# Moving the decay polynomial to GpSimd and regrouping the first products behind the attention

## The chip, the cores and the metric

One core of a Trainium2 chip runs the whole program in one launch. TensorE (PE) does the matmuls, VectorE (DVE), ScalarE (ACT) and GpSimd (POOL) work on data in SBUF, and DMA queues (here those of SP and ACT) move data from and to HBM. The time is that of the device in microseconds, from launch to end. The profile shows one execution of the same program.

## What is computed

A forgetting attention over 4 x 8 heads of 576 positions and 64 dimensions, then two feed-forward layers over the 2304 tokens; in short:

```python
log_f = np.log(np.clip(f, 0.0001, 1.0))
cum = np.cumsum(log_f, axis=-1)
decay = cum[:, :, :, None] - cum[:, :, None, :]
scores = np.where(causal, -1e9, q @ k.T / sqrt(D) + decay)
x = softmax(scores) @ v                 # to 2304 x 512
h = x @ w_in;  x = (h * tanh(log1p(exp(h)))) @ w_out
out = ((x @ w1) * (x @ w2)) @ w3 @ w_out2
```

All numbers are float32 to the reader, but the matmuls work on pairs: every operand is split into a hi part and a lo part (what the rounding of hi left), and three products hi*hi, hi*lo, lo*hi (`MM_PAIRS`) stand for one.

## The kernel before

**The start.** `phase_a` writes an order out by hand for ScalarE, VectorE and SP (`manual_schedule`); GpSimd's order is left to the scheduler. The weights arrive as 64-bit words. Each block of 128x512 goes through four steps: a load on SP (`cv_load`, L122), a rescaling of the exponent on ScalarE (`cv_exp`, L133), three bit operations on VectorE (`cv_bits`, L141 to L143, together a conversion), and the split: a cast to hi on ScalarE (L98) and a subtraction for lo on VectorE (L102), or later on GpSimd (L112). The list `first` holds ten such blocks in this order: t00, o0 to o3, t01, o4 to o7 (t is w3, o is the second w_out); `NEAR` of them are loaded ahead of the decays, and the first softmax is put behind the conversion with index `HOLD`. The blocks that come after (w3h of 44 us among them) are converted in the slots.

The decays are made by `decay_log` and `decay_rows`: the clipped f is split into mantissa and exponent, log of the mantissa is a polynomial in z = s*s (L264 to L267 on VectorE, ten operations on 128x144), then come the term of the exponent (L268, L269), a running sum (L279, a scan) and its rounding to pairs (L282 to L288). Four stores on SP (L290) write them to `cum_scr`, from which `load_cum` (L342 to L347) brings them as rows of `aug`, two more contraction rows of the attention's score products on TensorE (L371).

**The slots.** From there the attention runs in slots, in which TensorE alternates scores (L371, L374), transposes (L438, L442), products with v (L472) and a filler: the units of w3 times w_out (L521) and of the first layer's x @ w_in (L552). `misc` holds loads and splits by slot; up to slot 2 they are kept behind the last load of the start (`go_sp`).

**The boundary.** The filler ends with the first eight of the layer's products done for most tokens; the last block of tokens runs in `first_layer` by a scheme with seven products o = 1 to 7 for each of eight units m (Strassen and Winograd). Each product takes an x operand (TX, made by `x_operands`: sums on VectorE, cast on ScalarE, lo on VectorE L955) and a weight: products 1, 2 and 4 use the weights `wi` as they are, products 5, 6, 3 and 7 use `sp`, sums of weight quarters made on VectorE (`s_sums`, L1122 to L1127) and split by `s_build` (hi on ScalarE L1134, lo on VectorE L1135). The results are added into C: by ScalarE for products 1, 5 and 6 (L1070 to L1074) and by VectorE for 2, 3 and 7 (L1076 to L1080). `m_order` gives the order of the products; the operands are made ahead or behind a product by `hook`.

Of the kernel before, what the change touches and what calls it, by code (L numbers as in the profile page):

```python
# [43 lines left out]
NEAR = 4  # L44
# [31 lines left out]
class Kernel:  # L76
# [172 lines left out]
    def decay_log(self):  # L249
# [14 lines left out]
        dve.tensor_scalar(q, z, 1.0 / 17, None, ALU.mult)  # L264
        for k in (15, 13, 11, 9, 7, 5, 3):
            dve.scalar_tensor_tensor(q, q, 1.0 / k, z, ALU.add, ALU.mult)
        dve.scalar_tensor_tensor(q, q, 1.0, s, ALU.add, ALU.mult)  # L267
# [4 lines left out]
    def decay_rows(self, between, after):
# [38 lines left out]
    def zeros(self):  # L311

        nc = self.nc
        for i in range(2):
            nc.vector.memset(f32(self.aug[i]), 0.0)
            for r in (0, 64):
                nc.gpsimd.memset(f32(self.aug[i][r:r + 4, 0:S]), 1.0)
                nc.gpsimd.memset(f32(self.aug[i][r:r + 4, S:LAST if r else 2 * S]), 1.0)
            nc.gpsimd.memset(f32(self.aug[i][64:68, 2 * S:KQ]), 1.0)
            nc.gpsimd.memset(self.raw[i][0:64, 2 * S:2 * S + 64], 0.0)  # L320
            nc.gpsimd.memset(self.raw[i][64:128, LAST:2 * S], 0.0)
            nc.gpsimd.memset(self.pt4[i][64:128], 0.0)
            nc.gpsimd.memset(self.vb[i][64:128], 0.0)
# [277 lines left out]
    def phase_a(self):  # L601
# [16 lines left out]
        def go(i):  # L618
            self.cv_exp(first[i][0])
            self.last = self.cv_bits(first[i][0])  # L620

# [3 lines left out]
        self.consts()  # L625
# [1 line left out]
        with self.tc.manual_schedule(engines={getattr(mybir.EngineType, e) for e in ("Activation", "DVE", "SP")}):
# [708 lines left out]
```

## Time and profile before

| what | value |
|---|---|
| median of three runs | 924.03 us (926.38, 923.31, 924.03) |
| profiled execution | 920.79 us, of which 919.0 us span |
| mean granted TensorE clock | 0.991 |
| TensorE busy | 873.7 us (95%) |
| VectorE, ScalarE, GpSimd busy | 688.1, 483.3, 166.2 us |

The busy shares are averages over the whole span. To judge a change in one stretch, read the stretch itself: which engine was idle there, what ended its idle time, and what that releaser had been doing until then. A timeline line gives the begin of a group of like instructions, its length, the engine, the line of the kernel, the tiles written and read, and in brackets how long the engine stood idle before and whose work ended that. The end of a matmul is modelled, so the begin of the next one is the better mark.

### The profile page before, as it was taken

The page shows a single profiled execution, that of the slowest core. Times are in us where ns is not written, and L with a number is a line of the kernel's source. Part 1 is how long each engine was busy: PE and PEld are TensorE (multiplying, and loading weights), DVE is VectorE, ACT ScalarE, POOL GpSimd, SP SyncE. Part 2 cuts the span into 40 slices and gives each one's busy share as a digit, 9 for nine tenths or more (in the row PEclk, how much of TensorE's full clock was granted, in tenths as well). Part 3 has the DMA queues.
Part 4 walks back from the last instruction along what each step waited for, and adds up shares of the span by engine and source line. Part 5 has one row for each costly group of instructions (what it writes and reads, how often), then busy time and mean ns, then how long its engine had stood idle before and what let it go on. Part 6 is the DMA issues. An engine that isn't in the chain of part 4 may idle for free.

```text
span 919.0 us, 17491 instructions
## 1 busy us (share of the span) xinstructions
PE 873.7 (95%) x6338; PEld 806.1 (88%) x6338; DVE 688.1 (75%) x1361; ACT 483.3 (53%) x1035; POOL 166.2 (18%) x253
## 2 busy tenths in 40 slices
PE   2799999999999989799999999999999999999998
PEld 1577778888888758799999999999999999999998
DVE  8987796744767676788888889888788887544483
ACT  3766667655556454655645455455784545322152
POOL 4043333325778740000000000000000000000000
PEclk9899999999999999999999999999999999999999
DMA  6965567757788872244475549988986555555552
GB/s 186 273 193 171 174 195 223 214 159 231 247 274 277 286 239 89 70 138 138 138 229 161 184 165 337 368 316 296 413 303 190 153 168 169 161 164 166 174 166 78
DMA packets 129191, 190.12 MB, mean 207 GB/s; under 512 B 12352, under 2 KB 70736, under 8 KB 129104
## 3 DMA queue, kind: packets, MB, share of 16 engines
q1 hardware_dynamic: 114608, 172.66, 58.2%
q10 hardware_dynamic: 14496, 16.33, 5.8%
q8 instruction: 50, 0.82, 0.4%
q14 instruction: 37, 0.30, 0.1%
HBM read 131.44 MB, written 57.52 MB: 206 GB/s over the span
## 4 chain that ended last, share of the span: by engine, by line
PE 63%; DMA 7%; DVE 7%; POOL 5%; issue 2%; ACT 1%; SPq 0%; ACTq 0%; DVEq 0%; POOLq 0%
PE ps_x L993 15%; PE ps_x L1065 14%; PE ps_z L1065 7%; PE ps_l L552 6%; PE ps_z L993 6%; PE ps_y L993 6%; PE ps_y L1065 3%; DMA ws<-ws 2%; PE ps_s L371 2%; PE ps_s L472 2%; POOL pt L849 2%; DMA ws<-pt 1%; PE ps_t L438 1%; POOL pt L848 1%; DVE TX L955 1%
## 5 line engine op out<-in xcount | busy, mean ns | idle before, releaser
L552 PE MATMUL ps_l<-x,wi 128*128 128x288 f32 x696 | 103.2, 302 | 0.6 <-ACT h L556 0.6
L552 PEld LDWEIGHTS ps_l<-x,wi 128*128 128x128 f32 x696 | 94.8, 190 | 5.7 <-issue 2.8
L954 ACT CAST g_h<-y 128x576 fp32r<-128x576 f32 x96 | 63.6, 675 | 55.0 <-PE ps_x L993 26.1
L993 PE MATMUL ps_x<-g_h,ws 128*128 128x288 f32 x512 | 91.5, 297 | 0.9 <-ACT g_h L954 0.7
L955 DVE TENSOR_TENSOR g_l<-y,g_h 128x576 fp32r<-128x576 f32 x96 | 72.3, 753 | 16.1 <-ACT g_h L954 15.3
L401 ACT ACTIVATE P<-P,sum 128x256 f32<-128x256 f32 (+3 forms) x112 | 70.5, 631 | 24.7 <-DVE sum L391 14.6
L993 PEld LDWEIGHTS ps_x<-g_h,ws 128*128 128x128 f32 x512 | 75.8, 189 | 1.8 <-ACT g_h L954 1.2
L391 DVE CUSTOM_DVE_ANT_0 P<-ps_s,m 128x256 f32<-128x256 f32 (+2 forms) x96 | 48.4, 553 | 18.9 <-PE ps_s L371 18.9
L993 PE MATMUL ps_x<-g_l,ws 128*128 128x288 f32 x256 | 55.2, 297 | 0.5 <-DVE g_l L955 0.5
L453 DVE COPY pt<-ps_t 128x128 f32<-128x128 f32 (+1 forms) x64 | 29.7, 485 | 34.5 <-PE ps_t L438 33.8
L1065 PE MATMUL ps_x<-T,gs 128*128 128x288 f32 x384 | 53.8, 295 | 0.9 <-ACT Cg L1070 0.9
L371 PE MATMUL ps_s<-raw 64*128 64x128 f32 (+3 forms) x256 | 46.6, 476 | 8.3 <-DMA raw<-in_qk_dram 5.9
L1065 PE MATMUL ps_x<-T,ws 128*128 128x288 f32 x384 | 53.8, 295 | 0.0
L1065 PEld LDWEIGHTS ps_x<-T,gs 128*128 128x128 f32 x384 | 51.8, 188 | 1.1 <-ACT Cg L1070 1.1
L1065 PEld LDWEIGHTS ps_x<-T,ws 128*128 128x128 f32 x384 | 51.9, 188 | 0.0
L521 PE MATMUL ps_l<-wo,w3h 128*128 128x512 f32 x128 | 45.3, 423 | 5.2 <-DVE wo L102 4.0
L954 ACT CAST h_h<-ab 128x576 fp32r<-128x576 f32 x48 | 31.7, 673 | 34.0 <-PE ps_x L993 19.9
L993 PE MATMUL ps_x<-h_h,ws 128*128 128x288 f32 x256 | 46.3, 297 | 1.5 <-DMA ws<-ws 1.4
L955 DVE TENSOR_TENSOR h_l<-ab,h_h 128x576 fp32r<-128x576 f32 x48 | 35.9, 754 | 15.6 <-ACT h_h L954 15.5
L472 PE MATMUL ps_s<-pt,va 128*64 128x320 f32 (+3 forms) x384 | 45.0, 383 | 0.0
L438 PE MATMUL ps_t<-ident,P 128*128 128x128 f32 x288 | 40.2, 275 | 2.5 <-ACT pt L453 2.2
L993 PEld LDWEIGHTS ps_x<-g_l,ws 128*128 128x128 f32 x256 | 41.2, 189 | 1.0 <-DVE g_l L955 1.0
(278 smaller groups left out, 2180.0 us busy)
## 6 DMA issues: line engine op xcount, KB each, us to landing
ws<-ws SPq DMA_DIRECT2D x112, 512.0 KB
ws<-gs SPq DMA_DIRECT2D x84, 256.0 KB
ws<-pt SPq DMA_DIRECT2D x45, 256.0 KB
h_scr<-h ACTq DMA_DIRECT2D x64, 144.0 KB
y<-h_scr SPq DMA_DIRECT2D x16, 576.0 KB
cvrt<-in_w3t_dram SPq DMA_DIRECT2D x16, 512.0 KB
cvri<-in_w_in_dram SPq DMA_DIRECT2D x16, 512.0 KB
cvru<-in_w_out_dram SPq DMA_DIRECT2D x16, 512.0 KB
```

The source lines that it names most:

```text
L371: mm(ps[:, 512 * hh:512 * hh + n], t[r, q0:q0 + 128], t[r, 0:n], start=first, stop=not first)
L391: dve = ttr(P[hh][:, :n], ps[:, 512 * hh:512 * hh + n], self.m1[:, 512 - n:], -0.125, 3.0e38, ALU.add, ALU.min, st[hh])
L401: ins = nc.scalar.activation(t[:, :n], t[:, :n], AF.Exp, bias=b, scale=-1.0, accum_out=self.sums[:, i:i + 1])
L438: tr(self.ps_t[hh][:, o + 128 * k:o + 128 * k + 128], P[:, 128 * k:128 * k + 128], self.ident)
L453: return copy(dst[:, 0:c + 1, 128 * c:128 * c + 128], src)
L472: mm(ps[64 * hh:64 * hh + 64, 256 + q:256 + q + w], lhs, rhs, start=i == 0, stop=i == len(plan) - 1)
L521: mm(o, w, x, start=i == 0, stop=i == 23)
L552: mm(o[:, :TB], w, x, start=i == 0, stop=i == 11)
L954: self.mark(self.nc.scalar.copy(hi, raw))
L955: self.mark(self.nc.vector.tensor_tensor(lo, raw, f32(hi), ALU.subtract))
L993: mm(ps[:, r, :TB], w[:, 256 * a + 128 * e:256 * a + 128 * e + 128], ops[i][b][:, r], start=o in (1, 5, 2) and f == 0 and (a, b) == (0, 0) ...
L1065: mm(bank[:, r, :TB], w[:, i:i + 128], T[o, k][:, b, r], start=o in (1, 2, 5) and (k, a, b) == (0, 0, 0), stop=(k, a, b) == (1, 1, 0), ski ...
```

## The change

The decays: the polynomial goes to GpSimd as eight TENSOR_SCALAR and eight TENSOR_TENSOR operations of 128x144; VectorE keeps the exponent, the last addition (2q + e) and the scan, which now stand behind the conversions t00, o0 and o1. GpSimd joins the hand-written order: constants of the first pair, polynomial, masks, constants of the second pair. The loads t00 and o0 go ahead of q and k on SP, the four stores of the decays alternate between SP's and ScalarE's queue, `NEAR` and `HOLD` go from 4 to 6, and loads up to slot 8 are kept behind the start's. The boundary: `x_order` puts products 1 and 2 of units 0 and 1 ahead of the ones that need `sp`, and operands and sums are made in the matching order.

```diff
-HOLD = 4
+HOLD = 6
-NEAR = 4
+NEAR = 6
...
-    def decay_log(self):
+    def decay_log(self, after):
...
         nc.sync.dma_start(x, self.f)
+        after()
...
-        dve.tensor_scalar(q, z, 1.0 / 17, None, ALU.mult)
-        for k in (15, 13, 11, 9, 7, 5, 3):
-            dve.scalar_tensor_tensor(q, q, 1.0 / k, z, ALU.add, ALU.mult)
-        dve.scalar_tensor_tensor(q, q, 1.0, s, ALU.add, ALU.mult)
         dve.tensor_scalar(e, e, 126.0, 0.6931471805599453, ALU.subtract, ALU.mult)
-        dve.scalar_tensor_tensor(q, q, 2.0, e, ALU.mult, ALU.add)
-        self.lf = q
+        pool = nc.gpsimd
+        pool.tensor_scalar(q, z, 1.0 / 17, 1.0 / 15, ALU.mult, ALU.add)
+        for k in (13, 11, 9, 7, 5, 3, 1):
+            pool.tensor_tensor(q, q, z, ALU.mult)
+            pool.tensor_scalar(q, q, 1.0 / k, None, ALU.add)
+        pool.tensor_tensor(q, q, s, ALU.mult)
+        self.lf = q, e
...
-        dve.tensor_tensor_scan(cum, self.lf, self.lf, 0.0, ALU.add, ALU.bypass)
+        lf, e = self.lf
+        dve.scalar_tensor_tensor(lf, lf, 2.0, e, ALU.mult, ALU.add)
+        dve.tensor_tensor_scan(cum, lf, lf, 0.0, ALU.add, ALU.bypass)
...
-            nc.sync.dma_start(self.cum_scr[:, :, 144 * i:144 * i + 144], f32(slot[32 * i:32 * i + 32]))
+            (nc.sync, nc.scalar)[i % 2].dma_start(self.cum_scr[:, :, 144 * i:144 * i + 144], f32(slot[32 * i:32 * i + 32]))
...
-        with self.tc.manual_schedule(engines={getattr(mybir.EngineType, e) for e in ("Activation", "DVE", "SP")}):
+        engines = {getattr(mybir.EngineType, e) for e in ("Activation", "DVE", "SP", "Pool")}
+        with self.tc.manual_schedule(engines=engines):
+            self.consts()
             self.zeros()
-            self.decay_log()
+            self.blanks(0)
+            self.ones(0)
+            self.decay_log(lambda: early(0, 2))
             self.load_raw(0)
-            early(0, NEAR)
-            self.decay_rows(lambda: go(0), lambda: early(NEAR, NEAR + 1))
+            early(2, NEAR)
+            self.masks()
+            self.blanks(1)
+            self.ones(1)
+            exp(0)
+            for i in range(3):
+                bits(i)
+                if i:
+                    fin(i - 1)
+            self.decay_rows(lambda: fin(2), lambda: early(NEAR, NEAR + 1))
...
-                with self.behind(self.go_sp if s < 2 else None):
+                with self.behind(self.go_sp if s < 8 else None):
...
+    def x_order(self):
+        seq = self.m_order(8)
+        return [(0, 1), (0, 2), (1, 1), (1, 2), (0, 5), (0, 6), (0, 3), (0, 7), (1, 5), (0, 4), (1, 6), (1, 3)] + [
+            (m, o) for m, o in seq[seq.index((1, 3)) + 1:]]
...
+        self.x_operands(T, (1, 2))
         self.s_sums(0)
-        self.x_operands(T, (1, 5))
+        self.x_operands(T, (5,))
         self.s_build(0, 0)
-        self.x_operands(T, (6, 2))
+        self.x_operands(T, (6,))
         self.s_build(0, 1)
         cover()
+        sums = {(1, 2): 1, (1, 6): 2}
+        sums.update({(m, 6): m + 1 for m in range(2, 7)})
+        builds = {(0, 6): (1, 0), (0, 3): (1, 1), (1, 3): (2, 0), (1, 7): (2, 1)}
+        builds.update({(m, o): (m + 1, i) for m in range(2, 7) for i, o in enumerate((2, 3))})
```

(`blanks` and `ones` are the memsets of GpSimd that stood in `zeros`, one pair of buffers at a time; `masks` is the second half of `consts`.)

VectorE in the start, from the polynomial on (`lg` are the decays' tiles, `cu` the running sum, `cvt` and `cvo` blocks of w3 and w_out being converted, `w3l` and `wo` their lo parts). Before:

```order
L264 TENSOR_SCALAR lg_152<-lg_152 128x144
L266 SCALAR_TENSOR_TENSOR lg_152<-lg_152 128x144 x7
L267 SCALAR_TENSOR_TENSOR lg_152<-lg_152,lg_151 128x144
L268 TENSOR_SCALAR lg_151<-lg_151 128x144
L269 SCALAR_TENSOR_TENSOR lg_152<-lg_152,lg_151 128x144
L279 SCALAR_TENSOR_TENSOR cu_185<-lg_152 128x144
L141 TENSOR_SCALAR cvt_189<-cvt_189 128x512
L142 SCALAR_TENSOR_TENSOR cvt_189<-cvrt_177,cvt_189 128x512
L143 SCALAR_TENSOR_TENSOR cvt_189<-cvrt_177,cvt_189 128x512
```

and in the changed kernel (L282 is the last addition, L283 the scan):

```order
L141 TENSOR_SCALAR cvt_195<-cvt_195 128x512
L142 SCALAR_TENSOR_TENSOR cvt_195<-cvrt_134,cvt_195 128x512
L143 SCALAR_TENSOR_TENSOR cvt_195<-cvrt_134,cvt_195 128x512
L141 TENSOR_SCALAR cvo_197<-cvo_197 128x512
L142 SCALAR_TENSOR_TENSOR cvo_197<-cvro_136,cvo_197 128x512
L143 SCALAR_TENSOR_TENSOR cvo_197<-cvro_136,cvo_197 128x512
L102 TENSOR_TENSOR w3l_208<-cvt_195,w3h_207 128x512
L141 TENSOR_SCALAR cvo_202<-cvo_202 128x512
L142 SCALAR_TENSOR_TENSOR cvo_202<-cvro_167,cvo_202 128x512
L143 SCALAR_TENSOR_TENSOR cvo_202<-cvro_167,cvo_202 128x512
L102 TENSOR_TENSOR wo_0_216<-cvo_197,wo_0_216 128x512
L282 SCALAR_TENSOR_TENSOR lg_132<-lg_132,lg_131 128x144
```

Ten operations of the polynomial are gone, and the last addition and the scan have moved behind two more conversions and two splits.

TensorE at the boundary (`ps_x0`, `ps_x1`, `ps_y` and `ps_z` are PSUM banks, `TXo` the x operand of product o in its two halves, `wi0` and `wi1` the weights of units 0 and 1, `sp0` and `sp1` their sums). Before:

```order
L1065 MATMUL ps_x0_3927<-TX1_0_3945,wi0_1184 128x288 x6
L1065 MATMUL ps_x0_3927<-TX1_1_3950,wi0_1184 128x288 x6
L1065 MATMUL ps_z_3930<-TX5_0_3955,sp0_0_3933 128x288 x6
L1065 MATMUL ps_z_3930<-TX5_1_3960,sp0_0_3933 128x288 x6
L1065 MATMUL ps_x0_3927<-TX6_0_3967,sp0_0_3933 128x288 x6
L1065 MATMUL ps_x0_3927<-TX6_1_3972,sp0_0_3933 128x288 x6
L1065 MATMUL ps_y_3929<-TX2_0_3977,wi0_1184 128x288 x6
L1065 MATMUL ps_y_3929<-TX2_1_3982,wi0_1184 128x288 x6
L1065 MATMUL ps_z_3930<-TX3_0_4093,sp0_1_3934 128x288 x6
L1065 MATMUL ps_z_3930<-TX3_1_4098,sp0_1_3934 128x288 x6
L1065 MATMUL ps_x0_3927<-TX7_0_4116,sp0_1_3934 128x288 x6
L1065 MATMUL ps_x0_3927<-TX7_1_4123,sp0_1_3934 128x288 x6
```

and in the changed kernel:

```order
L1101 MATMUL ps_x0_3934<-TX1_0_3945,wi0_1191 128x288 x6
L1101 MATMUL ps_x0_3934<-TX1_1_3950,wi0_1191 128x288 x6
L1101 MATMUL ps_y_3936<-TX2_0_3955,wi0_1191 128x288 x6
L1101 MATMUL ps_y_3936<-TX2_1_3960,wi0_1191 128x288 x6
L1101 MATMUL ps_x1_3935<-TX1_0_3945,wi1_1195 128x288 x6
L1101 MATMUL ps_x1_3935<-TX1_1_3950,wi1_1195 128x288 x6
L1101 MATMUL ps_y_3936<-TX2_0_3955,wi1_1195 128x288 x6
L1101 MATMUL ps_y_3936<-TX2_1_3960,wi1_1195 128x288 x6
L1101 MATMUL ps_z_3937<-TX5_0_3972,sp0_0_3940 128x288 x6
L1101 MATMUL ps_z_3937<-TX5_1_3977,sp0_0_3940 128x288 x6
L1101 MATMUL ps_x0_3934<-TX6_0_3984,sp0_0_3940 128x288 x6
L1101 MATMUL ps_x0_3934<-TX6_1_3989,sp0_0_3940 128x288 x6
```

The products that take `wi` of both units have moved to the front, and those that take `sp0` behind them.

VectorE at the boundary, in the stretch ahead of the sums for unit 1 (`sr1`; `Cx_0` and `Cx_1` collect the results of units 0 and 1). Before:

```order
L955 TENSOR_TENSOR TX4_0_4143<-tmp_3937,TX4_0_4143 128x576
L955 TENSOR_TENSOR TX4_1_4148<-tmp_3937,TX4_1_4148 128x576
L1122 TENSOR_TENSOR sr1_0_4153<-wi1_1188 128x512
L1122 TENSOR_TENSOR sr1_1_4154<-wi9_1645 128x512
L1076 TENSOR_TENSOR Cx_0_4079<-Cx_0_4079,ps_y_3929 128x576
L1078 TENSOR_TENSOR Cx_0_4079<-Cx_0_4079,ps_z_3930 128x576
L1124 TENSOR_TENSOR sr1_2_4155<-sr1_1_4154 128x256
L1126 TENSOR_TENSOR sr1_3_4156<-sr1_0_4153,sr1_1_4154 128x256
L1080 TENSOR_TENSOR Cx_0_4079<-Cx_0_4079,ps_x0_3927 128x576
```

and in the changed kernel:

```order
L991 TENSOR_TENSOR TX3_1_4105<-xr15_3922,TX3_1_4105 128x288
L1112 TENSOR_TENSOR Cx_1_4123<-Cx_1_4123,ps_y_3936 128x576
L1158 TENSOR_TENSOR sr1_0_4164<-wi1_1195 128x512
L1158 TENSOR_TENSOR sr1_1_4165<-wi9_1652 128x512
L991 TENSOR_TENSOR TX4_0_4187<-tmp_3944,TX4_0_4187 128x576
L1139 TENSOR_TENSOR tmp_3944<-xr11_3219,tmp_3944 128x288
L1139 TENSOR_TENSOR tmp_3944<-xr15_3922,tmp_3944 128x288
L1114 TENSOR_TENSOR Cx_0_4086<-Cx_0_4086,ps_z_3937 128x576
L1160 TENSOR_TENSOR sr1_2_4166<-sr1_1_4165 128x256
L1162 TENSOR_TENSOR sr1_3_4167<-sr1_0_4164,sr1_1_4165 128x256
L1116 TENSOR_TENSOR Cx_0_4086<-Cx_0_4086,ps_x0_3934 128x576
```

An addition from `ps_y` (the result of unit 1's product 2) now stands ahead of these sums, and the operands of product 4 have moved between them.

## Rows read from the trace of the kernel before

**Rows 1.** Stages: us, busy per engine, PEclk the granted clock, DMA share, GB/s
```profile
20.75:44.00 23.25, 18.00 (x58) 12.22 (x58) 22.53 (x54) 16.31 (x41) 0.00 (x0) 0.85 0.96 280
...
50.00:260.00 210.00, 209.35 (x1488) 170.53 (x1488) 147.11 (x382) 132.70 (x386) 93.02 (x124) 1.00 0.66 201
...
364.72:391.29 26.57, 21.43 (x147) 20.74 (x145) 19.75 (x42) 17.08 (x34) 0.00 (x0) 0.94 0.22 70
```

**Rows 2.** Waits of TensorE, 0 to 50 us: total, times, longest
```profile
PE ps_s L371 <- DMA raw<-in_qk_dram: 5.9, 2, 5.2
...
PE ps_l L521 <- DVE wo L102: 4.0, 2, 2.3
```

**Rows 3.** Timeline of TensorE, start: begin, us, work [idle before <-releaser]
```profile
20.75 1.38 PE L371 MATMUL ps_s<-aug 64*128 64x128 f32 x4 [9.46 <-DMA aug<-cum_scr]
...
44.11 0.74 PE L521 MATMUL ps_l<-wo,w3h 128*128 128x512 f32 x2 [1.17 <-ACT w3h L98]
```

**Rows 4.** Chain that ended last, 200 to 256 us: begin, us, what
```profile
241.80 1.90 PE ps_s L371 x10
...
249.09 0.73 POOL pt L829
...
249.82 0.07 issue
```

**Rows 5.** Timeline of TensorE at the boundary
```profile
364.72 1.75 PE L1065 MATMUL ps_x<-TX,wi 128*128 128x288 f32 x12
...
369.97 1.88 PE L1065 MATMUL ps_x<-TX,sp 128*128 128x288 f32 x12 [1.92 <-ACT Cx L1070]
...
380.94 0.79 PE L1065 MATMUL ps_z<-TX,sp 128*128 128x288 f32 x4 [2.72 <-ACT sp L1134]
...
382.24 1.78 PE L1065 MATMUL ps_z<-TX,sp 128*128 128x288 f32 x8 [0.50 <-DVE sp L1135]
...
386.51 1.76 PE L1065 MATMUL ps_x<-TX,sp 128*128 128x288 f32 x12
...
391.29 1.76 PE L1065 MATMUL ps_x<-TX,sp 128*128 128x288 f32 x12
```

**Rows 6.** Timeline of VectorE at the boundary
```profile
375.95 0.74 DVE L1076 TENSOR_TENSOR Cx<-Cx,ps_y 128x576 f32<-128x576 f32 x1
...
381.50 0.68 DVE L1135 TENSOR_TENSOR sp<-sr,sp 128x512 fp32r<-128x512 f32 x1
```

**Rows 7.** Timeline of VectorE, start
```profile
6.13 0.23 DVE L264 TENSOR_SCALAR lg<-lg 128x144 f32<-128x144 f32 x1
...
9.07 0.67 DVE L268 TENSOR_SCALAR lg<-lg 128x144 f32<-128x144 f32 x1
...
10.12 0.46 DVE L279 TENSOR_TENSOR_SCAN cu<-lg 128x144 f32<-128x144 f32 x1
...
16.49 0.42 DVE L141 TENSOR_SCALAR cvo<-cvo 128x512 int32<-128x512 int32 x1
...
18.27 0.68 DVE L102 TENSOR_TENSOR wo<-cvo,wo 128x512 fp32r<-128x512 f32 x1
...
43.03 0.68 DVE L142 SCALAR_TENSOR_TENSOR cvt<-cvrt,cvt 128x512 int32<-128x512 int32 x1
...
44.56 1.11 DVE L143 SCALAR_TENSOR_TENSOR cvt<-cvrt,cvt 128x512 int32<-128x512 int32 x1
...
45.59 1.23 DVE L142 SCALAR_TENSOR_TENSOR cvt<-cvrt,cvt 128x512 int32<-128x512 int32 x1
```

**Rows 8.** GpSimd: two pieces of its timeline, and a group by line and shape
```profile
1.37 0.29 POOL L300 TENSOR_SCALAR_AFFINE_SELECT heads<-heads 128x128 f32<-128x128 f32 x1
...
44.21 4.35 POOL L112 TENSOR_TENSOR w3l<-cvt,w3h 128x256 fp32r<-128x256 f32 x4 [33.09 <-ACT w3h L98]
...
L829 POOL TENSOR_TENSOR pt<-cvu,cvu 128x256 f32<-128x256 f32 x8 | 5.8, 728 | 10.8 <-DVE cvu L143 10.8
```

**Rows 9.** Issues on SP's queue
```profile
13.85 2.58 SPq L290 DMA_DIRECT2D cum_scr<-cu  x4
```

More of the change, by code (lines that the diff above doesn't have):

```diff
@@ L301, in consts, with masks @@
                                     channel_multiplier=1)
+    def masks(self):
+        nc = self.nc
         nc.gpsimd.memset(self.m1, 0.0)
@@ L311, in zeros, with ones, blanks @@
     def zeros(self):
+        for i in range(2):
+            self.nc.vector.memset(f32(self.aug[i]), 0.0)
+    def ones(self, i):
         nc = self.nc
[L314 to L323, printed above, removed]
+        for r in (0, 64):
+            nc.gpsimd.memset(f32(self.aug[i][r:r + 4, 0:S]), 1.0)
+            nc.gpsimd.memset(f32(self.aug[i][r:r + 4, S:LAST if r else 2 * S]), 1.0)
+        nc.gpsimd.memset(f32(self.aug[i][64:68, 2 * S:KQ]), 1.0)
+    def blanks(self, i):
+        nc = self.nc
+        nc.gpsimd.memset(self.raw[i][0:64, 2 * S:2 * S + 64], 0.0)
+        nc.gpsimd.memset(self.raw[i][64:128, LAST:2 * S], 0.0)
+        nc.gpsimd.memset(self.pt4[i][64:128], 0.0)
+        nc.gpsimd.memset(self.vb[i][64:128], 0.0)
     def load_raw(self, p):
@@ L616, in early, with exp, bits @@
                 self.cv_load(first[i][0], first[i][1], where[i])
[L618 to L620 removed]
         def fin(i):
             first[i][2](*first[i][3:])
[L625 removed]
+        def exp(i):
+            if i < len(first):
+                self.cv_exp(first[i][0])
+        def bits(i):
+            exp(i + 1)
+            last = self.cv_bits(first[i][0])
+            if i == HOLD:
+                self.hold = last
         self.lo_eng = "dve"
[L627 removed]
+        engines = {getattr(mybir.EngineType, e) for e in ("Activation", "DVE", "SP", "Pool")}
+        with self.tc.manual_schedule(engines=engines):
+            self.consts()
             self.zeros()
[L629 removed]
+            self.blanks(0)
+            self.ones(0)
+            self.decay_log(lambda: early(0, 2))
             self.load_raw(0)
[L631 to L638 removed]
+            early(2, NEAR)
[8 more added lines that the diff above has]
+            self.decay_rows(lambda: fin(2), lambda: early(NEAR, NEAR + 1))
+            early(NEAR + 1, len(first))
+            for i in range(3, len(first)):
+                bits(i)
+                if i > 3:
+                    fin(i - 1)
             fin(9)
@@ L1055, in m_layer @@
         c = {}
-        for m, o in self.m_order(8):
+        for m, o in seq or self.m_order(8):
             if o == 1:
@@ L1166, in hook @@
         def hook(m, o):
-            if m == 0 and o in (1, 5, 6):
-                self.x_operands(T, ({1: 3, 5: 7, 6: 4}[o],))
-            if m < 7:
-                with self.between():
-                    if o == 6:
-                        self.s_sums(m + 1)
-                    elif o == 2:
-                        self.s_build(m + 1, 0)
-                    elif o == 3:
-                        self.s_build(m + 1, 1)
-            elif o == 6:
+            more = {(0, 1): 3, (1, 1): 7, (0, 5): 4}.get((m, o))
+            if more:
+                self.x_operands(T, (more,))
+            with self.between():
+                if (m, o) in sums:
+                    self.s_sums(sums[m, o])
+                if (m, o) in builds:
+                    self.s_build(*builds[m, o])
+            if (m, o) == (7, 6):
                 self.begun = self.k_begin("g0_", 8, self.y)
@@ L1190, in hook @@
                     self.v_convert(f - 1)
[L1192 removed]
+        self.m_layer("x", T, get, post, hook, self.x_order())
     def phase_b(self):
```

8 lines of the change are left out of this document (1 added, 7 removed).

## Prediction

> **What bounds the kernel now.** I read the table by stage first, then TensorE's waits at the start, then the timelines of the engines on which those waits end. From 50 to 260 us TensorE is busy 209.35 of 210 us, while in the start (20.75 to 44) it is busy 18.00 of 23.25 and at the boundary between attention and the next layer 21.43 of 26.57 [rows 1]. So the two places that the change edits are idle places of TensorE, 5.25 and 5.14 us, and in both the granted clock dips too (0.85 and 0.94) [rows 1].
>
> In the start TensorE waits 5.9 us for q and k and 4.0 us for weights that VectorE splits (L102) [rows 2], and 9.46 us for the decays (the loads of `aug` from `cum_scr`), till 20.75 [rows 3]. The decays come first in time. The later waits matter more, because what they leave is handed on: the last of them is 1.17 us at 44.11 for the hi part of w3's next block, whose words VectorE converts [rows 3]; from there TensorE is dense. VectorE is busy 22.53 of the 23.25 us [rows 1]. It is the bound of the start, and the length of its queue up to that conversion is what moves the end.
>
> The shift is carried to the end: the chain that ended last runs over TensorE's matmuls of the slots to 241.80 us and from there over VectorE to GpSimd's sums at 249.09 [rows 4], which follow the slots. I count a shift at 44 us as one to one.
>
> At the boundary TensorE waits 1.92 us at 369.97, 2.72 us at 380.94 (for the hi half of `sp` of unit 1) and 0.50 us at 382.24 (its lo half, L1135) [rows 5]. VectorE forms the sums that these need without a break, and its L1135 for unit 1 starts at 381.50 [rows 6].
>
> **Part A, the start.** *Removed from VectorE:* the polynomial (L264 to L267), from 6.13 to 9.07, 2.94 us [rows 7]. *Added in VectorE's queue:* near 44 us the order of the conversions changes: L142 of the second block now stands ahead of L143 of the first, which the cast for 44.11 needs. One L142 takes 0.68 us [rows 7], so +0.7 us. Without side effects: -2.3 us.
>
> *Added on GpSimd:* 16 operations of 128x144, each needing the one before. The trace of before has no such operation. GpSimd's nearest rows: an affine select of 128x128 (one input) 0.29 us, and a TENSOR_TENSOR of 128x256 728 ns on the mean [rows 8], 0.41 if scaled by size. So eight at about 0.29 and eight at 0.41 to 0.50 (it need not scale to nothing), 5.6 to 6.3 us of work, with gaps of 0.07 between dependent ones (L829 to L830 at 249.82 [rows 4]) about 7 us. They start where L264 stood, at 6.1, and end near 13.3 if nothing disturbs them. GpSimd did its constants there, which now stand behind; it is otherwise idle for 33.09 us before 44.21 [rows 8], so those cost nothing; without that cover they would push the w3 lo parts.
>
> *What they run beside:* VectorE now does three conversions and two splits in that time, eleven operations on 128x512, most with two inputs from SBUF. What such a pair costs is shown at 44 us: L142, alone 0.68 us, takes 1.23 at 45.59, and L143 takes 1.11 at 44.56 (three such rows in all) [rows 7], beside four GpSimd operations that take 4.35 us, 1.09 each instead of 0.73 [rows 8]. VectorE loses about 0.49 us for each operation there, against a GpSimd operation of 0.73, that is 0.67 of its length. Polynomial: 0.67 x 6 us = 4.0 us if all of it met such operations; the eight with one input, the gaps and L141 with one input take from that. Lower end 0 (the halves pass each other), value 2.4 us, which is the eight two-input operations of 0.45 at 0.67. The polynomial itself stretches in the same proportion, to about 16.5 to 17, while VectorE reaches the step that needs it (L282, which waits for GpSimd) at 6.13 + 0.23 + three conversions of 1.78 + two splits of 0.68 [rows 7] + 2.4 = 15.5. Queued behind L282 are the scan, the third split and every later conversion. Wait: 0 to 1.6 us, value 0.4. Sum of A: -2.3 + 2.4 + 0.4 = **+0.5 us**, ends -2.3 and +3.3.
>
> What the Trainium skill says on this page speaks against the edit: "SBUF — State Buffer", section "Who interferes with whom", states that a VectorE instruction with two SBUF inputs and a GpSimd instruction that reads SBUF exclude each other for the whole instruction. By it the loss would be the whole of what overlaps, about 4.5 us for the two-input half and part of the rest, and A about +2.2. The rows at 44 us lie near it: three operations of 0.68 and four of 0.73 make 5.0 us one after the other, and the stretch took 4.35. A at +2.2 would give 925.7, still in the main case's range.
>
> *The decays.* They now come later: before, the scan stood at 10.12 and the stores began at 13.85 [rows 7, 9]; 3.73 us, of which 1.9 were a conversion that now stands elsewhere. With L282 at about 16 the stores begin near 18.7, and with two queues instead of one the 2.58 us of issues [rows 9] halve. TensorE's 20.75 becomes about 24.3, +3.5. It is not the bound as long as it stays below the 5.25 us of idle in that stretch [rows 1], so cost nothing; beyond it each microsecond costs one. The first softmax is held two conversions longer (HOLD 6 for 4) under the same cover. The earlier loads (NEAR) and the loads kept behind the start's queue up to slot 8 lie on SP ahead of use by slots; the dense 209.35 of 210 us [rows 1] covers them, and if they came too late a wait like the 5.9 us for q and k [rows 2] would show.
>
> **Part B, the boundary.** Before, seven products stand ahead of the long wait, with 1.92 us idle among them. Now eight stand there, the first four of them without any `sp`, and all operands come in time by VectorE's order; one product takes (391.29 - 386.51) / 3 = 1.59 us [rows 5], so TensorE runs from 364.72 to 377.5 and then waits once for `sp` of unit 1. VectorE forms it later: the ps_y add of unit 1 (0.74 us, like that of unit 0 [rows 6]) now stands ahead of it, and I allow 0.4 for the first ps_y add waiting for ScalarE's copy of the first product (0 to 0.7; no row shows it). Release +1.1, but five products instead of six follow until unit 2: 1.1 - 1.59 = **-0.5 us**.
>
> The clock: after the wait two products took 386.51 - 380.94 = 5.57 us with 0.50 idle, against 3.19 at full speed, so 1.9 us were lost to the lower level [rows 5]. The wait is longer now (4.6 us against 2.72), so I let it be lost again. Ends: -1.9 if the clock holds, +1.6 if as much is lost as in the start, 15% of 23.25 us = 3.5 [rows 1]. B: -2.4 to +1.1.
>
> **Sum.** The profiled execution took 920.79 us, 919.0 of them span. +0.5 and -0.5 leave it there. The three runs have a median of 924.03, 3.24 above it, so I put the change on the median: **924.0 us**.
>
> **Rivals.** A difference under 0.3%, 2.8 us, can't be told from no change here: 921.2 and 926.8 are the marks.
>
> *1. GpSimd's work passes beside VectorE's for free.* A is -2.3, B -0.5: 921.2; with the clock holding 919.3. For it: half of the operations have one input, and they are short. Against: the rows at 44 us.
>
> *2. Slower: the decays arrive too late.* The polynomial on GpSimd is a chain in which each operation waits in turn behind a VectorE operation of 0.68 us; 16 x 0.68 + 6 = 17 us from 6.1 would end it at 23, and VectorE, with all further conversions behind L282, would stand still from 15.5 on. It decides from where the polynomial ends after 17; at 19 the wait at L282 is 3.5 us instead of 0.4, A is +3.6 and the time 927.1. For it: the 1.09 for 0.73 us. Against: VectorE has pauses between its operations in which GpSimd gets in.
>
> *3. The boundary gives nothing back:* VectorE is its bound, and the longer idle keeps the clock down longer (+1.1). With A at +0.5: 925.6.
>
> *4. The edit at the boundary doesn't act,* because VectorE's order leaves the first four products waiting for operands. Then B is 0 to +1: 924.5 to 925.5, in the main case's range.
>
> **Chances.** Main case 0.45 (own range 922.5 to 926), rival 1 0.27, rival 2 0.17, rivals 3 and 4 together 0.11. Faster by over 0.3%: most of rival 1 and a little of the main case, 0.25. Slower by over 0.3%: most of rival 2 and a tail of rival 3, 0.17. The rest, 0.58, is no change. The range runs from 919.8 (rival 1 with half of the clock's gain) to 927.6 (rival 2).
>
> **What the profile after would show.** Part A is right if GpSimd's polynomial ends between 15 and 18 us, VectorE's L142 and L143 before 17 us are above 0.68, L282 starts at 15 to 17, and TensorE's dense stretch begins within 1 us of 44.1. Rival 1: the conversions' operations at 0.68 and the dense stretch near 42. Rival 2: an idle time of 2 us or more ahead of L282. Part B is right if the first eight products run without a gap, then one wait of 4 to 5 us, and unit 2 begins about 26 us after the boundary's first product. The forecast is wrong altogether if the stretch from 50 to 364 us changes its length, which I have taken as fixed.

## The result and the profile after

The changed kernel is slower: 929.24 us (median) against 921.51 us for the kernel before on the same chip, a ratio of 1.0067 (95% interval 1.0047 to 1.0088), that is 6 us, 4.3 to 8.1 (the two medians lie 7.7 us apart; I go by the ratio and its interval). I had forecast no change, on 924.03, the median of the first three of these fifteen runs of before: 924.0, and by the range -4.2 to +3.6 us. What came is slower, at the place that rival 2 names, to which I gave 0.17, and by more than its +3.1. One run of experiment 1 (1227.92 us, at a granted clock of 0.661 where its others have about 0.99) is left out of its ratio. The profiled execution took 927.56 us, 925.8 of them span.

The stages of the kernel after, to be laid beside [rows 1] (columns as there; the boundary now begins at 369.81, so the last row covers another part of it):

```profile
20.75:44.00 23.25, 12.91 (x52) 8.88 (x51) 22.00 (x54) 13.46 (x34) 3.86 (x11) 1.00 0.72 212
44.00:50.00 6.00, 3.65 (x13) 2.21 (x11) 5.97 (x14) 4.01 (x9) 1.08 (x2) 0.73 0.83 234
50.00:260.00 210.00, 209.11 (x1473) 170.79 (x1474) 141.66 (x372) 130.16 (x374) 91.56 (x121) 0.99 0.66 201
364.72:391.29 26.57, 22.14 (x152) 21.59 (x151) 24.24 (x54) 14.55 (x27) 0.00 (x0) 0.88 0.27 88
```

From 50 to 260 us TensorE is as dense as before (209.11 of 210). The loss lies ahead of that: 5.1 us less TensorE work fits between 20.75 and 44, while VectorE is as busy as it was. TensorE's timeline of the start, after (begin, length, [idle before]):

```profile
28.42 0.44 PE L385 MATMUL ps_s<-aug 64*128 64x128 f32 x1 [7.38 <-DMA aug<-cum_scr]
...
43.33 0.50 PE L535 MATMUL ps_l<-wo,w3h 128*128 128x512 f32 x1 [2.00 <-DVE wo L102]
...
48.83 0.73 PE L535 MATMUL ps_l<-wo,w3h 128*128 128x512 f32 x2 [2.01 <-ACT w3h L98]
...
55.95 0.73 PE L535 MATMUL ps_l<-wo,w3h 128*128 128x512 f32 x2
```

The decays arrive at 28.42 instead of 20.75, w3's second block at 48.83 instead of 44.11 [rows 3]: the dense stretch begins 4.7 us late. VectorE's timeline shows what it did until then:

```profile
3.33 0.48 DVE L257 TENSOR_SCALAR lg<-lg 128x144 f32<-128x144 f32 x1
3.85 0.57 DVE L258 TENSOR_SCALAR lg<-lg 128x144 int32<-128x144 int32 x1
...
4.45 0.66 DVE L260 CAST lg<-lg 128x144 f32<-128x144 int32 x1
...
6.66 0.31 DVE L264 TENSOR_TENSOR lg<-lg 128x144 f32<-128x144 f32 x1
...
8.21 0.86 DVE L143 SCALAR_TENSOR_TENSOR cvt<-cvrt,cvt 128x512 int32<-128x512 int32 x1
...
12.02 0.69 DVE L102 TENSOR_TENSOR w3l<-cvt,w3h 128x512 fp32r<-128x512 f32 x1 [0.89 <-ACT w3h L98]
...
14.70 0.78 DVE L102 TENSOR_TENSOR wo<-cvo,wo 128x512 fp32r<-128x512 f32 x1
19.54 0.31 DVE L282 SCALAR_TENSOR_TENSOR lg<-lg,lg 128x144 f32<-128x144 f32 x1 [4.06 <-POOL lg L271]
```

It came to L282 at 15.48 and stood there 4.06 us for the end of the polynomial, with every later conversion queued behind. GpSimd's timeline, in which L269 and L270 are the polynomial's product and addition:

```profile
4.38 0.64 POOL L327 MEMSET aug<- 4x576 f32 x1
...
7.14 0.47 POOL L267 TENSOR_SCALAR lg<-lg 128x144 f32<-128x144 f32 x1 [1.39 <-DVE lg L265]
7.70 0.82 POOL L269 TENSOR_TENSOR lg<-lg 128x144 f32<-128x144 f32 x1
8.61 1.06 POOL L270 TENSOR_SCALAR lg<-lg 128x144 f32<-128x144 f32 x1
...
18.37 0.57 POOL L270 TENSOR_SCALAR lg<-lg 128x144 f32<-128x144 f32 x1
19.02 0.49 POOL L271 TENSOR_TENSOR lg<-lg,lg 128x144 f32<-128x144 f32 x1
```

The polynomial runs from 7.14 to 19.51, 12.4 us; on VectorE it took 2.94. Beside VectorE's operations a product takes up to 0.83 and an addition 0.89 to 1.09 us; after VectorE has stopped, 0.49 and 0.57.

At the boundary TensorE did what I had written down:

```profile
369.81 1.76 PE L1101 MATMUL ps_x<-TX,wi 128*128 128x288 f32 x12
...
380.99 1.76 PE L1101 MATMUL ps_x<-TX,sp 128*128 128x288 f32 x12
387.17 3.58 PE L1101 MATMUL ps_z<-TX,sp 128*128 128x288 f32 x12 [4.42 <-ACT sp L1170]
390.55 2.41 PE L1101 MATMUL ps_x<-TX,wi 128*128 128x288 f32 x12
392.80 1.75 PE L1101 MATMUL ps_x<-TX,sp 128*128 128x288 f32 x12
...
397.58 1.76 PE L1101 MATMUL ps_x<-TX,wi 128*128 128x288 f32 x12
```

Eight products without a gap, then one wait. The two products after it take 5.63 us instead of 3.2, with the granted clock of the stretch at 0.88.

### The profile page after: what moved, and what is told of

The parts are those of the page before. It is cut to its first block, busy times and chain, and to the rows that moved or that the text cites. A ratio compares the mean times of both kernels' runs of the same rounds, so it can differ in the third digit from the quotient of the medians.

```text
span 925.8 us, 17512 instructions
## 1 busy us (share of the span) xinstructions
PE 872.2 (94%) x6338; PEld 805.4 (87%) x6338; DVE 683.3 (74%) x1352; ACT 483.4 (52%) x1035; POOL 177.8 (19%) x269
## 4 chain that ended last, share of the span: by engine, by line
PE 77%; DMA 9%; DVE 5%; POOL 4%; ACT 2%; issue 2%; SPq 1%; ACTq 0%; DVEq 0%; POOLq 0%
PE ps_x L1101 15%; PE ps_x L1029 15%; PE ps_z L1101 8%; PE ps_l L566 7%; PE ps_z L1029 6%; PE ps_y L1029 6%; PE ps_s L385 4%; PE ps_l L535 4%; PE ps_y L1101 4%; PE ps_s L486 3%; PE ps_t L452 2%; DMA ws<-ws 2%; DMA R<-inv_scr 2%; DMA cvri<-in_w_in_dram 2%; PE ps_s L388 1%
## 5 line engine op out<-in xcount | busy, mean ns | idle before, releaser
L991 DVE TENSOR_TENSOR h_l<-ab,h_h 128x576 fp32r<-128x576 f32 x48 | 35.9, 754 | 16.6 <-ACT h_h L990 16.5
```

The source lines that it names most:

```text
L991: self.mark(self.nc.vector.tensor_tensor(lo, raw, f32(hi), ALU.subtract))
```

## The experiments

Where the expectations name theories by letters, G is the theory that GpSimd's long polynomial holds VectorE up; Q is the one that the length of VectorE's queue up to w3's second block sets the end; O is the one that the late decays themselves set it. "The shift" is the begin of w3's second block on TensorE (48.83 after) less 44.11.

**1. The polynomial back on VectorE, all else as in the change.** (It is nine operations there, L264, seven times L266 and L267; the ten that I count ahead of the prediction and in the expectation are one too many.)

```diff
-        pool.tensor_scalar(q, z, 1.0 / 17, 1.0 / 15, ALU.mult, ALU.add)
...
+        dve.tensor_scalar(q, z, 1.0 / 17, None, ALU.mult)
+        for k in (15, 13, 11, 9, 7, 5, 3):
+            dve.scalar_tensor_tensor(q, q, 1.0 / k, z, ALU.add, ALU.mult)
+        dve.scalar_tensor_tensor(q, q, 1.0, s, ALU.add, ALU.mult)
```

> The changed kernel with one thing undone: the polynomial stands on VectorE again, in its old ten operations, at the same place (ahead of the first three conversions); order of loads and conversions, queues, NEAR, HOLD and the boundary stay changed. Theory G (GpSimd's chain is the cost): in the changed kernel VectorE stands idle for 4.06 us ahead of L282 and loses about 1.5 us to slower operations beside GpSimd; both go, the 2.94 us of the polynomial come back, so the dense stretch of TensorE begins 2.5 to 3 us sooner than in the changed kernel (46 instead of 48.83), and the time falls by 3 to 5 us. Rival O (the order is the cost: decays behind three conversions, so that TensorE's first aug product comes at 28.4 instead of 20.75): the decays are still late by some 4 us and the time falls by under 1.5 us.

Measured: 1.0026 of before (0.9999 to 1.0053): 0.41%, 3.8 us, less than the change (about 0.1 to 0.75%, worked out from the two intervals). TensorE's start there:

```profile
25.20 0.44 PE L383 MATMUL ps_s<-aug 64*128 64x128 f32 x1 [6.92 <-DMA aug<-cum_scr]
...
46.00 1.22 PE L533 MATMUL ps_l<-wo,w3h 128*128 128x512 f32 x2 [2.51 <-ACT w3h L98]
```

The wait at the last addition is gone and the shift falls from 4.7 to 1.9 us, although VectorE again does 2.9 us of work more. So the move to GpSimd is most of the loss, by the middles; the interval leaves room for less. Some 2 us of shift stay, and the decays still come 4.5 us late.

**2. The two halves of the change apart.** First the start alone (the boundary as before), then the boundary alone (the start as before), and the latter once more.

```diff
...
-        self.m_layer("x", T, get, post, hook, self.x_order())
+        self.m_layer("x", T, get, post, hook)
```

(In this edit and the next the order of the operands and sums goes with this line.)

> The changed kernel's start with the boundary of the kernel before. Theory G, with the boundary worth what its rows say (after against before, 5.09 us late at the first product and 4.70 at unit 2): 0.4 us longer than the changed kernel, 6 to 7.5 us over the kernel before. Rival B (the longer idle of 4.4 us at the boundary costs by a lower clock, or the new order there): 1 us or more shorter than the changed kernel.

```diff
...
-        self.m_layer("x", T, get, post, hook)
+        self.m_layer("x", T, get, post, hook, self.x_order())
```

> The kernel before with the boundary's new order alone. Theory G: 0.4 us shorter than the kernel before, so no difference that can be seen; one wait of 4 to 5 us in place of waits of 1.9, 2.7 and 0.5. Rival B: 1 us or more longer.

> The kernel before with the boundary's new order alone, once more, for its sign: e3 gave 0.9986 (0.9961 to 1.0011). By the rows 0.4 to 0.5 us less (0.9995); by the median of e3 1.1 to 1.3 us less (0.9986). Over 1.001 would go against both.

Measured: start alone 1.0063 (1.0042 to 1.0085), boundary alone 0.9986 (0.9961 to 1.0011) and 0.9963 (0.9939 to 0.9988). The start is the whole loss. The boundary alone is faster than the kernel before by 1.3 us in one set of runs and by 3.4 in the other: its sign rests on the second, since the first interval reaches past 1, and its size stays open. Behind the changed start no gain of it is seen: 1.0067 with it, 1.0063 without. TensorE with the boundary alone, first set:

```profile
365.53 1.76 PE L1071 MATMUL ps_x<-TX,wi 128*128 128x288 f32 x12
...
382.89 3.58 PE L1071 MATMUL ps_z<-TX,sp 128*128 128x288 f32 x12 [4.43 <-ACT sp L1140]
...
393.36 1.76 PE L1071 MATMUL ps_x<-TX,wi 128*128 128x288 f32 x12
```

From the first product to unit 2 (393.36) it takes 27.83 us, after 27.77, and before 28.16 (364.72 [rows 5] to 392.88). But the old order in the kernel with the start alone took 26.84 (372.04 to 398.88): there two products at 377.29 and 380.08 were slow (2.99 and 2.20 us) ahead of the wait for `sp`, which was 1.45 us instead of 2.72, and none behind it. The trace of single executions doesn't settle 1 us here.

**3. What the polynomial costs on GpSimd with nothing beside it.** The scan and what follows it stand ahead of all conversions, so VectorE does nothing meanwhile.

```diff
             exp(0)
-            for i in range(3):
-                bits(i)
-                if i:
-                    fin(i - 1)
-            self.decay_rows(lambda: fin(2), lambda: early(NEAR, NEAR + 1))
+            self.decay_rows(lambda: None, lambda: early(NEAR, NEAR + 1))
...
```

> The changed kernel with the last addition, the scan and the stores of the decays ahead of all conversions, so that VectorE has nothing to do beside GpSimd's polynomial: what the chain costs by itself. From the last seven of its operations in the changed kernel, when VectorE stood idle (0.57 and 0.49 us, 0.08 between): 8 x 0.65 + 8 x 0.57 = 9.8 us instead of 12.4. If operations beside it cost it nothing (a rival to the contention of my prediction), it stays at 12.4. VectorE idle some 9.5 us, conversions at 0.69, and the dense stretch 2 to 3 us later than in the changed kernel.

Measured in a single execution: 932.09 us. GpSimd's groups by line, then the first and last piece of the polynomial in the timeline:

```profile
L270 POOL TENSOR_SCALAR lg<-lg 128x144 f32<-128x144 f32 x7 | 4.0, 570 | 0.6
L269 POOL TENSOR_TENSOR lg<-lg 128x144 f32<-128x144 f32 x7 | 3.4, 487 | 0.6
```

```profile
7.15 0.31 POOL L267 TENSOR_SCALAR lg<-lg 128x144 f32<-128x144 f32 x1 [1.40 <-DVE lg L265]
...
16.14 0.49 POOL L271 TENSOR_TENSOR lg<-lg,lg 128x144 f32<-128x144 f32 x1
```

Alone it is 9.5 us long (7.15 to 16.63), where I had allowed 7; the work beside it adds 2.9 to make the 12.4 of after. The products cost what I had bounded (0.49). The additions cost 0.57, twice my price of 0.29, and yet L267, the same instruction with a multiplication and an addition in one, takes 0.31.

**4. Why an addition costs 0.57.** Two edits, each made to the changed kernel by itself: the addition written with two operations (times 1.0, plus 1/k), and the product written to another tile, so that the addition no longer works in place.

```diff
-            pool.tensor_scalar(q, q, 1.0 / k, None, ALU.add)
+            pool.tensor_scalar(q, q, 1.0, 1.0 / k, ALU.mult, ALU.add)
```

> The changed kernel with seven of GpSimd's TENSOR_SCALAR operations written as times 1.0 plus 1/k instead of plus 1/k alone. In the run with nothing beside, the one that is written with two operations took 0.31 us and the seven with one took 0.57. Theory F (the form counts): 0.31 for all, the chain ends some 1.8 us sooner (17.6 instead of 19.45), VectorE waits 2.2 instead of 4.06 us at L282. Rival I (writing in place counts: the first reads another tile than it writes): no change.

```diff
-            pool.tensor_tensor(q, q, z, ALU.mult)
-            pool.tensor_scalar(q, q, 1.0 / k, None, ALU.add)
+            pool.tensor_tensor(u, q, z, ALU.mult)
+            pool.tensor_scalar(q, u, 1.0 / k, None, ALU.add)
```

> The changed kernel with GpSimd's products written to a second tile, so that no TENSOR_SCALAR of it reads the tile that it writes. Rival I: 0.31 us for each of the seven, the chain ends near 17.6. Theory F: 0.57 as before, the chain ends at 19.4.

Measured in a single execution each: 926.33 and 934.63 us, which says nothing of the time (the fifteen runs of the changed kernel lie between 922.35 and 933.41). With two operations, GpSimd's last addition and then VectorE's wait:

```profile
17.03 0.31 POOL L270 TENSOR_SCALAR lg<-lg 128x144 f32<-128x144 f32 x1
```

```profile
17.94 0.31 DVE L282 SCALAR_TENSOR_TENSOR lg<-lg,lg 128x144 f32<-128x144 f32 x1 [2.71 <-POOL lg L271]
```

It is the form: 0.31 with two operations, 0.57 with the addition alone, in place or not (the other tile left the wait at 4.06). A multiplication alone was not run. The polynomial ends 1.6 us sooner, the wait falls by 1.35 and the shift by 1.3. That is G at another dose, and it doesn't reach zero. But the kernel with the other tile, whose wait is that of the changed one, has w3's second block at 47.86, and the two boundary-alone runs have it at 44.14 and 44.89: single executions scatter by up to 1 us in the shift, so of the three the wait is the safe reading.

**5. Take the wait away instead.** First the last addition and the scan behind five conversions instead of three; then this with the two-operation form and GpSimd's first memsets behind the polynomial; then that with `NEAR` 8.

```diff
-            for i in range(3):
+            for i in range(5):
...
-            self.decay_rows(lambda: fin(2), lambda: early(NEAR, NEAR + 1))
+            self.decay_rows(lambda: fin(4), lambda: early(NEAR, NEAR + 1))
...
```

> The changed kernel with the last addition, the scan and the stores of the decays two conversions later (behind five instead of three), so that VectorE has work while GpSimd's polynomial runs. Theory Q (what counts is VectorE's queue: the 4.06 us that it stood idle at L282 are handed on to the dense stretch): the idle time goes to under 0.5, TensorE's first aug product comes no sooner than in the changed kernel (28.4, rather 29), and still the product with w3's second block moves from 48.83 to 45 to 46 and the time falls by 3 to 4 us. Rival O (the late decays and so TensorE's late start at 28.4 are what counts): it stays at 48 or later and the time within 1 us of the changed kernel's.

> The changed kernel with three changes at once: the two-operation form of f2, the later scan of f1, and the memsets of the first pair behind the polynomial on GpSimd, so that they don't run beside VectorE's first operations (0.17 to 0.32 us in the kernel before, 0.17 to 0.66 in the changed one, 0.87 us later at z). Theory Q with theory F: no idle time at L282, and 0.9 us gained at the begin: w3's second block at 44 to 45, the time within 2 us of the kernel before, to either side. Rival O: the first aug product still after 27 us, w3's second block at 47 or later, 4 us or more over the kernel before.

```diff
-NEAR = 6
+NEAR = 8
```

> The mended start of f4 with two more loads ahead of the decays' stores on SP (NEAR 8 for 6). In f1 and f4 the idle time of VectorE at L282 was gone, but 3.7 and 3.9 us of it came back behind it, waiting for o4, whose load stands on SP behind the stores of the decays. Theory Q (VectorE's queue sets the dense stretch): the wait for o4 falls below 1 us and w3's second block moves from 50.95 to 47 to 48, the time falls by 3 to 4 us against f4; it stays over the kernel before, since 2.2 us of waiting for the cast at 12.35 and the slower operations beside GpSimd remain. Rival O (late decays): w3's second block stays at 50 or later.

Measured: 1.0104 (1.0076 to 1.0131), 1.0098 (1.0067 to 1.0130) and 1.0069 (1.0043 to 1.0095). The second block of w3 comes at 51.53, 50.95 and 48.77 us. None gains on the changed kernel, against what Q says of the first two. In these L282 no longer waits, but VectorE stands later, for a block of w_out. Its timeline in the second, and SP's issue of the load behind that:

```profile
30.93 0.43 DVE L141 TENSOR_SCALAR cvo<-cvo 128x512 int32<-128x512 int32 x1 [3.86 <-ACT cvo L133]
```

```profile
26.30 0.59 SPq L122 DMA_DIRECT2D cvro<-in_wo_dram  x1
```

That load stands on SP behind the decays' stores (24.96 there), which now come later: the wait has only moved. With `NEAR` 8 it stands ahead of the stores. VectorE's one long wait before 14 us, its waits from 14 to 50 (total, times, longest), then lines of ScalarE and of TensorE, SP's issue of the load that ScalarE waits for there, and the same issue in the kernel before:

```profile
12.10 0.75 DVE L102 TENSOR_TENSOR w3l<-cvt,w3h 128x512 fp32r<-128x512 f32 x1 [1.51 <-ACT w3h L98]
```

```profile
DVE pt L467 <- PE ps_t L452: 3.9, 1, 3.9
DVE cvo L141 <- ACT cvo L133: 0.2, 1, 0.2
DVE cu L286 <- PE ps_l L284: 0.2, 1, 0.2
```

```profile
42.45 0.70 ACT L133 ACTIVATE cvt<-cvrt 128x512 f32<-128x512 f32 x1 [3.37 <-DMA cvrt<-in_w3t_dram]
...
45.53 0.70 ACT L415 ACTIVATE P<-P,sum 128x512 f32<-128x512 f32 x1
```

```profile
30.59 1.30 PE L385 MATMUL ps_s<-aug 64*128 64x128 f32 x4 [7.84 <-DMA aug<-cum_scr]
...
47.50 1.54 PE L452 MATMUL ps_t<-ident,P 128*128 128x128 f32 x6 [4.01 <-ACT pt L467]
```

```profile
34.84 0.59 SPq L122 DMA_DIRECT2D cvrt<-in_w3t_dram  x1
```

```profile
30.81 0.37 SPq L122 DMA_DIRECT2D cvrt<-in_w3t_dram  x1
```

Now VectorE has one wait of 1.51 us at 12.10 and none worth the name from there to 45, where it is ahead and stands 3.9 us for TensorE itself; the time is still that of the change, 0.3% under that of the second, which the intervals don't tell from nothing. The decays come at 30.59, 9.8 us late, and with them everything on SP behind them: w3's load is issued at 34.84, four us later than in the kernel before. ScalarE stands 3.37 us for it with the softmax of the slot queued behind, and TensorE waits 4.01 for the transposes that need that softmax. So in this trace, with VectorE free, the lateness of the decays sets the end, through SP's and ScalarE's queues.

**6. Are the 4.5 us of lateness that the kernel of experiment 1 keeps harmful too?** That kernel with the decays' last steps and stores ahead of all conversions but one:

```diff
-            for i in range(3):
-                bits(i)
-                if i:
-                    fin(i - 1)
-            self.decay_rows(lambda: fin(2), lambda: early(NEAR, NEAR + 1))
+            self.decay_rows(lambda: bits(0), lambda: early(NEAR, NEAR + 1))
...
```

> The run e1 (polynomial on VectorE) with the last addition, the scan and the stores of the decays ahead of the conversions again, one conversion between, as in the kernel before; loads, NEAR, HOLD, queues and GpSimd's order stay changed. Theory Q: VectorE's queue has the same work, so although TensorE's first aug product comes at about 21 instead of 25.2, w3's second block stays at 45.4 to 46 and the time within 1 us of e1. Rival O: w3's second block at 44.5 or sooner and the time 1.5 us or more under e1.

Measured: 1.0022 (0.9996 to 1.0048), as in experiment 1. TensorE:

```profile
19.64 1.30 PE L383 MATMUL ps_s<-aug 64*128 64x128 f32 x4 [7.98 <-DMA aug<-cum_scr]
...
45.28 1.22 PE L533 MATMUL ps_l<-wo,w3h 128*128 128x512 f32 x2 [0.81 <-ACT w3h L98]
```

The decays come 5.6 us sooner than there, sooner even than before, and w3's second block only 0.7 us, which is within the scatter; the runs can't tell the two times apart. So 4.5 us late costs next to nothing, as I had argued from the 5.25 us of idle time, while by the trace of experiment 5 9.8 does. By these traces neither Q nor O holds alone; each binds where the other is out of the way.

**7. What is left in experiment 1's kernel.** In it as in the change, GpSimd's memsets stand at the very front, beside VectorE's first operations. Here the long ones of the first pair (4x576) go behind the masks and the short ones:

```diff
-            self.blanks(0)
-            self.ones(0)
             self.decay_log(lambda: early(0, 2))
...
             self.masks()
+            self.blanks(0)
             self.blanks(1)
+            self.ones(0)
             self.ones(1)
```

> The run e1 (polynomial on VectorE) with GpSimd's long memsets of the first pair behind the others, where they don't run beside VectorE's first operations. Theory M (these memsets slow VectorE's TENSOR_SCALAR and CAST): L257 to L261 back to 0.17 to 0.32 us as in the kernel before, z some 0.9 us sooner, w3's second block at 45.1 instead of 46.00, the time 1 us under e1. Rival: they stay at 0.48 to 0.66, and nothing moves.

Measured: 0.9999 (0.9974 to 1.0024). VectorE, then TensorE:

```profile
3.33 0.17 DVE L257 TENSOR_SCALAR lg<-lg 128x144 f32<-128x144 f32 x1
3.54 0.23 DVE L258 TENSOR_SCALAR lg<-lg 128x144 int32<-128x144 int32 x1
...
3.88 0.22 DVE L260 CAST lg<-lg 128x144 f32<-128x144 int32 x1
...
5.75 0.31 DVE L264 TENSOR_TENSOR lg<-lg 128x144 f32<-128x144 f32 x1
```

```profile
44.33 1.22 PE L533 MATMUL ps_l<-wo,w3h 128*128 128x512 f32 x2 [2.24 <-ACT w3h L98]
```

L257, L258 and L260 are back from 0.48, 0.57 and 0.66 to 0.17, 0.23 and 0.22, z is there 0.91 us sooner, and the shift is 0.2. The trace shows the cause; the times of experiments 1 and 7 (2.5 us apart) have intervals that overlap. With the polynomial and the memsets undone no loss is left that the runs can tell: the ratio is 0.68% under that of the change (about 0.35 to 1.0%, from the two intervals). The boundary's new order is in this kernel too, and what it gains may cover a rest.

## Why the prediction was wrong

**The length of the polynomial** is the step that failed. I had it start at 6.1, last 7 us by itself, stretch to end at 16.5 to 17, and VectorE wait 0.4 us. It started at 7.14 (+1.0), is 9.5 us by itself (+2.5) and was stretched by 2.9 (I had allowed 3.4 to 3.9): it ended at 19.51. The price that was most off is that of the one-input operation. I took it from an affine select, 0.29 us [rows 8]; the eighth of them costs that (L267, 0.31), the seven with a single operation cost 0.57, 2.0 us more in all. The 16 operations and 15 gaps of 0.08 make up the rest. I carried both ends of the two-input price into the range and none for the one-input price, which rested on an operation of another kind. In place of the 0.4 us that I gave the wait at L282, VectorE stood there 4.06.

**The late start** I had costed at nothing. I spoke of GpSimd's idle time as cover for its memsets, but not of what they do to VectorE. The hint stood in [rows 7]: L268, a TENSOR_SCALAR of 128x144, took 0.67 where L264, of the same form, took 0.23. Beside it, in the kernel before, ran on GpSimd:

```profile
9.09 0.57 POOL L318 MEMSET aug<- 4x576 f32 x1
```

I passed over it; it is the price that L257, L258 and L260 paid in the changed kernel.

**VectorE's loss beside GpSimd** I set at 2.4 us. It is about 0.8 up to L282 (three L143 at 0.86 for 0.69, two L141 at 0.52, one split at 0.78). Still VectorE came to L282 at 15.48, as forecast (15.5), by luck, as two errors cancel: less contention, but the late start and 0.89 us of waiting for ScalarE's cast at 12.02. What VectorE didn't lose, GpSimd did: 0.82 for 0.49 and 0.89 to 1.09 for 0.57, while VectorE's operations grew by a quarter at most. The Trainium skill ("SBUF — State Buffer", section "Who interferes with whom") has such a pair contend for a shared port pair that is an exclusive lock; the sum by it, with whole instructions lost on VectorE, would have been A at +2.2. The trace agrees that they collide, but hardly on VectorE's side, and the loss came from the chain of waits instead.

**Rival 2** named the place (L282), the wait and the point ("at 19 the wait is 3.5 us, A is +3.6"). The polynomial ended at 19.51 and the wait was 4.06. Its reason for the late end was not the one found: it had each operation wait behind one of VectorE's, 16 times 0.68, and an end at 23; the stretch is 2.9 us in all, less than the main case allowed, and the chain's own length and its late start make the rest. Its "against", that GpSimd gets in between VectorE's operations, fits that small stretch and was not enough. As measured, A's sum is -2.9 (polynomial) + 0.7 (order of conversions) + 0.8 (contention) + 4.1 (L282) + 0.9 (start) + 0.9 (cast) + 0.3 (the load at 25.27, 0.66 for 0.33) + 0.4 (L292 beside a memset, 0.67 for 0.23) = 5.2; the shift is 4.7, and the half microsecond that is left over I have not traced.

**One to one.** The time grew by 4.3 to 8.1 us for 4.7 of shift, by 7 to 12 in the kernel with the scan later for 7.4, by 2.4 (0 to 5) in experiment 1 for 1.9. One to one is inside each interval, though the middles lie near 1.3. Between the two profiles it holds as far as the next layer: TensorE is 5.09 us later at the boundary's first product, 4.70 at unit 2 and 4.66 at 561.86 (557.20 before). The spans differ by 6.8; the other 2.1 come behind that: from there to TensorE's last products it is 359.7 us and was 357.6, and in the profiles of the other runs this stretch scatters from 357.7 to 361.0. A difference that the clock made in the start did not last: from w3's block to the products at 55.95 it is 7.1 us and was 5.5 (44.11 to 49.63), with a granted clock of 0.73 on the mean from 44 to 50, where it was 1.00, and two matmuls of w3h in 1.05 us instead of 0.62 (1.2 instead of 2.4 GHz); by the boundary only 0.4 of that 1.6 is left. One pair of profiles can't show the rule, though. From w3's block to the boundary's first product it is 320.6 us before and 321.0 after, but up to 328.3 in the other runs: 321.9 on the mean of the three profiles with the start of before, 323.9 of the eleven with the changed one. Whether the new start also lengthens the slots by a microsecond or two stays open.

**The decays' slack** of 5.25 us fits experiments 6 and 5: 4.5 us late costs next to nothing, 9.8 does. In the changed kernel they are 7.7 late (I had 3.5; the stores began at 22.97 instead of 18.7, behind the wait at L282), so by my own rule 2.4 us of it were over the slack and not free. That they bind by SP's queue, on which w3's and w_out's loads stand behind them, I had not seen: I had checked the loads ahead of the decays only. No run kept the 7.7 and took the wait at L282 away, so what each is worth in the changed kernel itself stays open.

**Part B** was right in its mechanism. The release of unit 1's product 5 moved from 16.22 to 17.36 us behind the first product (+1.14; forecast +1.1), the wait is 4.42 (4.6), the lower clock fell on the two products behind it again, and first product to unit 2 is 0.39 shorter in the trace (0.5). The mark that I gave for it, unit 2 about 26 us after the first product, was a slip: [rows 5] and the sum of -0.5 make it 27.7 (28.16 before, to the product at 392.88), and it is 27.77. In time B is worth 1.3 to 3.4 us with the start of before, inside or beyond the end of -2.4 that I gave it, and nothing that the runs can tell with the changed start. It couldn't make up for A. A slip without weight: rival 1 with half of the clock's gain is 920.25 and not 919.8, the lower end of my range.

## What to carry to other kernels

A chain of small dependent operations moved to an idle engine must be priced as a chain: every operation's own form, its gap, and the stretch beside the engine that is relieved; then compare its end with the moment at which that engine needs the result, for what waits there is the whole queue and not the operation. Price it with rows of the same form only, and keep both ends for every row that is not. When a result gets later, look also at what stands behind its stores and loads on the DMA queue: in experiment 5 the late decays reached TensorE through the loads behind them.

## What the hardware showed that I had not expected

- On GpSimd a TENSOR_SCALAR of 128x144 takes 0.57 us with an addition alone and 0.31 with a multiplication and an addition; a TENSOR_TENSOR takes 0.49, with 0.08 between dependent ones. The Trainium skill ("GPSIMD Engine Reference", section "Engine selection") calls GpSimd near line rate with one input and half as fast with two; here the one-input form with an addition alone is slower than the two-input one, and the measurement decides.
- A GpSimd memset of 4x576, which reads nothing, slows VectorE's TENSOR_SCALAR and CAST of 128x144 from 0.17 to 0.23 us to 0.48 to 0.66 (L257, L258, L260), and leaves its RECIPROCAL at 1.05. Not every one is hit: L261 in the changed kernel stayed at 0.17, and in experiment 7 a TENSOR_SCALAR at 6.15 took 0.19 while the memset beside it took 0.77 instead of 0.57. The Trainium skill ("SBUF — State Buffer", section "Who interferes with whom") says that `cast` and `tensor_scalar` can take the ports that VectorE shares with GpSimd; the trace agrees.
- Where VectorE's two-input operations and GpSimd's meet in the changed kernel, the loss is uneven: 0.69 to 0.86 on VectorE, 0.49 to 0.82 and 0.57 to 1.09 on GpSimd.
- After the boundary's wait of 4.4 us TensorE ran on at the lower of its two clocks (1.2 instead of 2.4 GHz): two products took 5.63 us instead of 3.2, and 5.67 in the boundary-alone kernel. Shorter waits did not always have it, nor the same wait in every execution: after 1.9 us at the same place of the old order a product took 1.88 us in the kernel before (369.97) and 2.99 in the kernel with the start alone (377.29).
